# A SwiGLU feed-forward kernel: one weight load moves from SyncE's queue to GpSimd, behind a wait

## The chip, the core and the metric

The kernel runs on one core of a Trainium2 chip. The metric is the device time of one execution in microseconds (us), as a median over several executions. In the profile PE is TensorE's matmuls, PEld its weight loads, DVE is VectorE, ACT is ScalarE, POOL is GpSimd and SP is SyncE; a name with q behind it (SPq, POOLq) is that engine's instruction queue, which also issues DMAs.

## What is computed

```python
B, S, D, F = 1, 2048, 512, 1376     # all bfloat16

def reference(x, w_gate, w_up, w_down):
    g = silu(x @ w_gate)             # [2048, 1376]
    u = x @ w_up                     # [2048, 1376]
    return (g * u) @ w_down          # [2048, 512]
```

## The kernel before

The 2048 tokens are worked in four chunks of 512, numbered c = 0 to 3. F is cut into tiles of 128 columns: ten whole tiles (0 to 9) and a rest of 96. Each whole tile of each chunk has a gate group G and an up group U. A group accumulates over four slices of D (the loop variable `dk`) into one PSUM bank of 128 partitions by 512 columns. Each product is issued as two matmuls, one for each half of the 128 output partitions (`m` is 0 or 64). ScalarE takes silu of the gate bank into `sg_sb` (L291), and VectorE multiplies it with the up bank into `hT_sb` (L305). When all four chunks are through, the rests of F are worked (kinds X and Y), and then the down projection with `wd_sb` gives the output rows, which SyncE stores.

The order of groups on TensorE is written out in the plan: for each chunk tile 0, tile 1, then tiles 2 and 3 together (both gates, then both ups), then tiles 4 to 9 one by one. Chunk 0 has a special beginning: its first 256 tokens arrive untransposed in `xn_sb`, TensorE transposes them (L374, L382), and tiles 0 and 1 are computed in pieces of 256 and 128 tokens as the parts of x arrive. From the gates of tile 2 on every matmul is 512 columns wide.

The weights lie in `w_sb`. They are loaded in slabs: `slabs = [(0, 2), (2, 4), (4, 6), (6, 8), (8, NFT)]`, where the pair is the first tile and the one behind the last. Slab a has one load of gate columns, named `wg` with its first tile (wg0, wg2, wg4, wg6, wg8), and one of up columns (wu0, wu2 and so on); `load_w` (L98) issues either. A load of two tiles is 256 KB: 128 partitions, four slices of D, 512 bytes each. Each load has a semaphore of its own that reaches 16 when all of it has landed. Before its first matmul with a load TensorE waits for that semaphore (`need`, L317 and in `gu_step`).

The DMA issues before the change, each engine's in the order of its queue:

- ScalarE: wg0, ahead of its first activation.
- SyncE: the untransposed x (`xn`, L114), wu0, two transposing loads of x for the rest of chunk 0 (x0b and x0c, L93), wg2, wu2, wg4, wu4, wg6, wu6, wg8, wu8, a small load wut, the transposing loads x1, x2 and x3 of the other chunks, the down weights (wd, four wdt, wdl), and much later the stores of the output.
- GpSimd: no DMA. It makes one iota (L274), from which VectorE makes the identity for the transposes.

There are no loops at run time; all queues are written out when the program is built.

Of the kernel before, what the change touches and what calls it, by code (L numbers as in the profile page):

```python
# [13 lines left out]
def bass_standalone__swiglu_ffn__prompt_kernel(nc, x, w_gate, w_up, w_down, out):  # L14
    _, S, D = x.shape
    F = w_gate.shape[1]
    P = 128
# [29 lines left out]
    with ExitStack() as es:  # L47
# [33 lines left out]
        loads = {}  # L81

        def load_sem(name):
            loads[name] = sem(f"s_{name}")
            return loads[name]
# [6 lines left out]
        def load_x(eng, name, t0, t1):  # L92
            eng.dma_start_transpose(  # L93
                xT_sb[:, :, t0:t1], xf[t0:t1, :]
            ).then_inc(load_sem(name), 16)

        def load_w(eng, name, src, base, f0, f1):
            eng.dma_start(  # L98
                w_sb[:, :, base + f0:base + f1],
                src[:, f0:f1].rearrange("(k p) f -> p k f", p=P),  # L100
            ).then_inc(load_sem(name), 16)

        slabs = [(0, 2), (2, 4), (4, 6), (6, 8), (8, NFT)]
        slab_of = {ft: a for a, b in slabs for ft in range(a, b)}

        def load_slab(eng, a, b):
            load_w(eng, f"wg{a}", w_gate, 0, a * P, min(b * P, F))
            load_w(eng, f"wu{a}", w_up, UPH, a * P, min(b * P, F - 32))

        def loads_on_scalar(act):  # L110
            load_w(act, "wg0", w_gate, 0, 0, slabs[0][1] * P)

        def loads_on_sync(sp):
            sp.dma_start(  # L114
                xn_sb[:, :, :].rearrange("p j d -> p (j d)"), xf[0:HT, :].rearrange("(p j) d -> p (j d)", j=NXN)
            ).then_inc(load_sem("xn"), 16)
            load_w(sp, "wu0", w_up, UPH, 0, slabs[0][1] * P)
            load_x(sp, "x0b", HT, HT + P)
            load_x(sp, "x0c", HT + P, SC)
            for a, b in slabs[1:]:  # L120
                load_slab(sp, a, b)
            load_w(sp, "wut", w_up, F - (F - 32), F - 32, F)
            for c in range(1, NSC):
                load_x(sp, f"x{c}", c * SC, (c + 1) * SC)
            sp.dma_start(
                wd_sb[:, 0:NFF, :], w_down[0:NFF * P, :].rearrange("(k p) d -> p k d", p=P)
            ).then_inc(load_sem("wd"), 16)
            for c in range(NSC):
                sp.dma_start(
                    wdt_sb[R * c:R * (c + 1), :, :], w_down[NFF * P:F, :].rearrange("(q p) d -> p q d", p=R)  # L130
                ).then_inc(load_sem(f"wdt{c}"), 16)
            sp.dma_start(wdl_sb[:, :], w_down[NFF * P:F, LASTA:D]).then_inc(load_sem("wdl"), 16)
# [86 lines left out]
        for dk in range(KD):  # L219
            g = add_group("T", dk=dk)  # L220
            eng = "DA"[dk % 2]
# [19 lines left out]
        for at in range(NST):  # L241
# [4 lines left out]
            for c0, c1 in [(0, LASTA), (LASTA, LASTB), (LASTB, D)] if end else [(0, D)]:  # L246
                g = add_group("O", t=t, c0=c0, c1=c1, c=c)
                (quads[j] if c0 == 0 else last).append(g)
                eng = "A" if (end and c0 == 0) or (j < TPC - 1 and c % 2) else "D"
                op = add_op(  # L250
                    eng, g, kind="copy", out=o_sb[ob][:, c0:c1], src=g["bank"][:, 0:c1 - c0],
# [6 lines left out]
        def rows_of(t):  # L258
            if t < NXN:
                return of[0:HT, :].rearrange("(p j) d -> j p d", j=NXN)[t]  # L260
            return of[t * P:(t + 1) * P, :]

        def on_sync(sp):
            loads_on_sync(sp)
            for t, c0, c1, ob, eng, n in stores:
                if (c0, c1) == (0, LASTA):
                    continue
                sp.wait_ge(s_A if eng == "A" else s_D, n)
                sp.dma_start(rows_of(t)[:, c0:c1], o_sb[ob][:, c0:c1]).then_inc(s_out[ob], 16)
            for i in range(NST, NST + NOS):  # L270
                sp.wait_ge(s_out[i % NOS], 16 * n_store[i % NOS])

        def on_gpsimd(pool):
            pool.iota(  # L274
                diag[:, :], pattern=[[-1, P]], base=0, channel_multiplier=1,
            ).then_inc(s_I, 1)

        def on_scalar(act):
            loads_on_scalar(act)
            act.activation(adummy[:, 0:4], zero_c, ACT.Silu)  # L280
            for op in act_ops:
                act.wait_ge(s_P, op["g"]["at"] + 1)
                if op["kind"] == "silu":
                    if op["free"]:
                        act.wait_ge(s_D, op["free"])
                    fn = ACT.Silu
                else:
                    if op["stored"][1]:
                        act.wait_ge(*op["stored"])
                    fn = ACT.Copy  # L290
                act.activation(op["out"], op["src"], fn).then_inc(s_A, 1)  # L291
            for t, c0, c1, ob, eng, n in stores:
                if (c0, c1) == (0, LASTA):
                    act.wait_ge(s_A, n)
                    act.dma_start(rows_of(t)[:, c0:c1], o_sb[ob][:, c0:c1]).then_inc(s_out[ob], 16)
# [215 lines left out]
                ).then_inc(s_P, 1)  # L511

        on_sync(nc.sync)
        on_gpsimd(nc.gpsimd)
        on_scalar(nc.scalar)
        on_tensor(nc.tensor)
        on_vector(nc.vector)

# [27 lines left out]
```

## Time and profile before

| what | value |
|---|---|
| three executions | 120.25, 119.51, 119.6 us; median 119.6 us |
| the profiled execution | 120.67 us, of which the profile's span is 119.3 us |
| PE busy | 116.6 us, 98% of the span |
| PEld, DVE, ACT busy | 66.4, 43.4, 35.5 us |
| POOL busy | 0.4 us, five instructions |
| HBM read | 4.81 MB |
| mean granted TensorE clock | 1.000 |

The span runs from the first to the last recorded instruction; what lies around it, here 1.4 us, belongs to the launch and the end of the execution. "Busy" for PE includes a matmul's modelled end, so that overlapping matmuls leave no gap even where they run slowly. DMA times are given from the start of the issuing instruction to the last landing.

### The profile page before, as it was taken

The page shows a single profiled execution, that of the slowest core. Times are in us where ns is not written, and L with a number is a line of the kernel's source. Part 1 is how long each engine was busy: PE and PEld are TensorE (multiplying, and loading weights), DVE is VectorE, ACT ScalarE, POOL GpSimd, SP SyncE. Part 2 cuts the span into 40 slices and gives each one's busy share as a digit, 9 for nine tenths or more (in the row PEclk, how much of TensorE's full clock was granted, in tenths as well). Part 3 has the DMA queues.
Part 4 walks back from the last instruction along what each step waited for, and adds up shares of the span by engine and source line. Part 5 has one row for each costly group of instructions (what it writes and reads, how often), then busy time and mean ns, then how long its engine had stood idle before and what let it go on. Part 6 is the DMA issues. An engine that isn't in the chain of part 4 may idle for free.

```text
span 119.3 us, 2992 instructions
## 1 busy us (share of the span) xinstructions
PE 116.6 (98%) x1343; PEld 66.4 (56%) x1344; DVE 43.4 (36%) x68; ACT 35.5 (30%) x61; POOL 0.4 (0%) x5
## 2 busy tenths in 40 slices
PE   7999999999999999999999999999999999999993
PEld 2796555555555555555555555554444444464452
DVE  0103534442534452444352444369800040214331
ACT  4225243265242365232454323470000030213001
POOL 1000000000000000000000000000000000000000
DMA  3999999991000000000000000000000023023612
GB/s 80 278 283 335 194 253 228 269 295 23 0 5 0 0 0 0 5 0 5 0 5 0 0 0 0 5 0 0 5 0 5 0 86 95 0 92 106 204 44 88
DMA packets 17596, 8.92 MB, mean 75 GB/s; under 512 B 8624, under 2 KB 17456, under 8 KB 17584
## 3 DMA queue, kind: packets, MB, share of 16 engines
q1 hardware_dynamic: 16912, 8.38, 27.1%
q10 hardware_dynamic: 672, 0.36, 1.0%
q8 instruction: 10, 0.16, 0.6%
q14 instruction: 2, 0.02, 0.0%
HBM read 4.81 MB, written 2.10 MB: 58 GB/s over the span
## 4 chain that ended last, share of the span: by engine, by line
PE 98%; issue 0%; DVE 0%
PE psum L345 59%; PE psum L456 24%; PE psum L433 7%; PE psum L409 3%; PE psum L359 2%; PE psum L420 1%; PE psum L382 0%; PE psum L374 0%; PE psum L364 0%; DVE o_sb L309 0%; PE psum L508 0%
## 5 line engine op out<-in xcount | busy, mean ns | idle before, releaser
L345 PE MATMUL psum<-xT_sb,w_sb 128*64 128x512 bf16 (+2 forms) x680 | 71.0, 371 | 0.0
L345 PEld LDWEIGHTS psum<-xT_sb,w_sb 128*64 128x64 bf16 x680 | 43.0, 112 | 27.1
L305 DVE TENSOR_TENSOR hT_sb<-sg_sb,psum 128x512 bf16<-128x512 f32 x40 | 27.5, 687 | 41.5 <-PE psum L345 36.6
L291 ACT ACTIVATE sg_sb<-psum 128x512 f32<-128x512 f32 x40 | 23.8, 596 | 41.6 <-PE psum L345 41.6
L456 PE MATMUL psum<-wd_sb,hT_sb 32*128 32x512 bf16 x480 | 26.9, 374 | 0.0
L456 PEld LDWEIGHTS psum<-wd_sb,hT_sb 32*128 32x128 bf16 x480 | 13.0, 93 | 13.0 <-issue 0.4
L309 DVE CAST o_sb<-psum 128x512 bf16<-128x512 f32 (+1 forms) x11 | 6.4, 603 | 25.2 <-PE psum L456 19.9
L291 ACT ACTIVATE o_sb<-psum 128x512 bf16<-128x512 f32 (+1 forms) x7 | 3.7, 580 | 33.0 <-PE psum L456 25.9
L433 PE MATMUL psum<-wd_sb,hT_sb 128*128 128x512 bf16 (+2 forms) x59 | 8.7, 307 | 0.2 <-issue 0.2
L433 PEld LDWEIGHTS psum<-wd_sb,hT_sb 128*128 128x128 bf16 x60 | 4.6, 98 | 4.6 <-issue 0.4
L305 DVE TENSOR_TENSOR ht_sb<-sgy_sb,yu_sb 32x512 bf16<-32x512 f32 x8 | 5.5, 683 | 0.4
L409 PE MATMUL psum<-xT_sb,w_sb 128*64 128x512 bf16 x32 | 4.2, 379 | 0.0
L305 DVE TENSOR_TENSOR ht_sb<-sgx_sb,psum 32x512 bf16<-32x512 f32 x4 | 2.8, 691 | 3.5 <-ACT sgx_sb L291 3.5
L291 ACT ACTIVATE sgx_sb<-psum 32x512 f32<-32x512 f32 x4 | 2.4, 588 | 4.5 <-PE psum L409 4.5
L359 PE MATMUL psum<-const-bfloat16-1.0 128*128 128x512 bf16 x6 | 2.7, 623 | 0.8 <-PEq L531 0.8
L456 PE MATMUL psum<-wdt_sb,ht_sb 32*128 32x512 bf16 (+1 forms) x48 | 3.3, 371 | 0.0
L409 PEld LDWEIGHTS psum<-xT_sb,w_sb 128*64 128x64 bf16 x32 | 2.0, 110 | 1.4
L291 ACT ACTIVATE sgy_sb<-psum 64x512 f32<-64x512 f32 x4 | 2.4, 590 | 0.1
L456 PEld LDWEIGHTS psum<-wdt_sb,ht_sb 32*128 32x128 bf16 x48 | 1.3, 93 | 1.3
L420 PE MATMUL psum<-xT_sb,w_sb 128*64 128x512 bf16 x16 | 1.9, 379 | 0.0
L359 PEld LDWEIGHTS psum<-const-bfloat16-1.0 128*128 128x128 bf16 x6 | 0.7, 133 | 1.9 <-issue 1.9
L280 ACT ACT_TABLE_LOAD x1 | 1.3, 1283 | 1.2 <-PEq L531 1.2
(21 smaller groups left out, 7.6 us busy)
## 6 DMA issues: line engine op xcount, KB each, us to landing
out_dram<-o_sb SPq DMA_DIRECT2D x15, 128.0 KB, 1.8
wd_sb<-in_w_down_dram SPq DMA_DIRECT2D x1, 1280.0 KB, 8.9
w_sb<-in_w_up_dram SPq DMA_DIRECT2D x4, 256.0 KB, 4.0
w_sb<-in_w_gate_dram SPq DMA_DIRECT2D x3, 256.0 KB, 3.9
wdt_sb<-in_w_down_dram SPq DMA_DIRECT2D x4, 96.0 KB, 7.2
w_sb<-in_w_gate_dram SPq DMA_DIRECT2D x1, 352.0 KB, 6.2
w_sb<-in_w_up_dram SPq DMA_DIRECT2D x1, 320.0 KB, 6.3
w_sb<-in_w_gate_dram ACTq DMA_DIRECT2D x1, 256.0 KB, 3.6
```

What stands on the lines that cost most here:

```text
L280: act.activation(adummy[:, 0:4], zero_c, ACT.Silu)
L291: act.activation(op["out"], op["src"], fn).then_inc(s_A, 1)
L305: ins = dve.tensor_tensor(op["out"], op["a"], op["b"], ALU.mult)
L309: ins = dve.tensor_copy(op["out"], op["src"])
L345: ins = pe.matmul(g["bank"][m:m + HC, n0:n1], lhsT=w_sb[:, dk, col + m:col + m + HC], rhs=xT_sb[:, dk, c * SC + n0:c * SC + n1], start=(dk ...
L359: pe.matmul(banks[NB - 1][:, 0:width], lhsT=ones_w, rhs=ones_m[:, 0:width], start=True, stop=True)
L409: ins = pe.matmul(g["bank"][m:m + HC, :], lhsT=w_sb[:, dk, XC0 + m:XC0 + m + HC], rhs=xT_sb[:, dk, c * SC:(c + 1) * SC], start=(dk == 0), ...
L420: ins = pe.matmul(g["bank"][y0:y1, :], lhsT=w_sb[:, dk, YC0:YC0 + 64], rhs=xT_sb[:, dk, c * SC:(c + 1) * SC], start=(dk == 0), stop=(dk == ...
L433: ins = pe.matmul(g["bank"][:, 0:c1 - c0], lhsT=hT_sb[:, fk, t * P:(t + 1) * P], rhs=wd_sb[:, fk, c0:c1], start=(start and fk == 0), stop= ...
L456: ins = pe.matmul(g["bank"][:, 0:c1 - c0], lhsT=h(r, g["t"]), rhs=w[R * r:R * (r + 1), c0:c1], start=(start and n == 0), stop=final, tile_ ...
```

## The change

The load wg2 leaves SyncE's queue. GpSimd issues it instead, behind its iota and behind a wait for wg0's semaphore to reach 16. SyncE goes from x0c straight to wu2. ScalarE's program is now built before GpSimd's, because wg0's semaphore is made there; each engine's own queue is otherwise as it was. The matmuls, their order and their waits by name are the same.

```diff
-        def load_slab(eng, a, b):
-            load_w(eng, f"wg{a}", w_gate, 0, a * P, min(b * P, F))
+        def load_slab(eng, a, b, gate=True):
+            if gate:
+                load_w(eng, f"wg{a}", w_gate, 0, a * P, min(b * P, F))
             load_w(eng, f"wu{a}", w_up, UPH, a * P, min(b * P, F - 32))
...
             for a, b in slabs[1:]:
-                load_slab(sp, a, b)
+                load_slab(sp, a, b, gate=a != slabs[1][0])
...
             pool.iota(
                 diag[:, :], pattern=[[-1, P]], base=0, channel_multiplier=1,
             ).then_inc(s_I, 1)
+            pool.wait_ge(loads["wg0"], 16)
+            load_w(pool, "wg2", w_gate, 0, slabs[1][0] * P, slabs[1][1] * P)
...
         on_sync(nc.sync)
+        on_scalar(nc.scalar)
         on_gpsimd(nc.gpsimd)
-        on_scalar(nc.scalar)
         on_tensor(nc.tensor)
         on_vector(nc.vector)
```

## The prediction

> **What bounds the kernel now.** I read the chain that ended last first, then TensorE's waits, then SyncE's queue in the first ten microseconds, then the moment at which the moved load is needed. The page says who sets the end:
>
> ```profile
> PE 116.6 (98%) x1343; PEld 66.4 (56%) x1344; DVE 43.4 (36%) x68; ACT 35.5 (30%) x61; POOL 0.4 (0%) x5
> ...
> PE 98%; issue 0%; DVE 0%
> ```
>
> The chain followed back from the last instruction is TensorE almost alone. Its waits, in the view of who waited for whom with PE alone:
>
> ```profile
> PE psum L359 <- PEq L531: 0.8, 1, 0.8
> PE psum L433 <- issue: 0.2, 1, 0.2
> ```
>
> Neither is a wait for a DMA: the first is the start of the program, the second is in the down projection. This view can hide a short wait under a matmul's modelled end, so I also followed the starts of the weight loads and matmuls one by one through the first 13 us. From 4.4 us on they follow one another without a hole. The one load that gates TensorE is wg0, and with it the transposed x: wg0 is issued at 0.73 and takes 3.6, so it lands at 4.33, and the first weight load of L345 starts at 4.39 (the last copy of x that it needs ends only shortly before, so both decide). From a landing to the weight load that waits for it there are thus 0.06 us.
>
> SyncE's queue in that time, as the timeline has it:
>
> ```profile
> 1.67 2.57 SPq L93 DMA_TRANSPOSE xT_sb<-in_x_dram  x2
> 4.28 0.58 SPq L98 DMA_DIRECT2D w_sb<-in_w_gate_dram  x1
> 4.91 0.51 SPq L98 DMA_DIRECT2D w_sb<-in_w_up_dram  x1
> 5.46 0.51 SPq L98 DMA_DIRECT2D w_sb<-in_w_gate_dram  x1
> ```
>
> The issue at 4.28 is wg2. The view of w_sb for the windows round this issue and round ScalarE's wg0 gives their landings (the last column of the first line is the form):
>
> ```profile
> L98 ACTq DMA_DIRECT2D w_sb<-in_w_gate_dram x1: 463/463/463, 0.7 to 0.7; - x1
> ...
> DMA to landing us min/median/max: 3.6/3.6/3.6
> ...
> L98 SPq DMA_DIRECT2D w_sb<-in_w_gate_dram x1: 581/581/581, 4.3 to 4.3; - x1
> ...
> DMA to landing us min/median/max: 3.5/3.5/3.5
> ```
>
> So wg2 lands at 4.28 + 3.55 = 7.83 (the landing records give the second digit). When is it needed? Its matmuls are the first that are 512 columns wide, and the groups by form between 9.07 and 9.10 us hold just the change from 256 to 512:
>
> ```profile
> L345 PE MATMUL psum<-xT_sb,w_sb 128*64 128x256 bf16 x4 | 0.4, 273 | 0.0
> L345 PE MATMUL psum<-xT_sb,w_sb 128*64 128x512 bf16 x2 | 0.4, 379 | 0.0
> ```
>
> The first of them starts at 9.08, and the weight load that carries the wait for wg2 at 8.97. It therefore lands 1.1 us before it is needed. This spare time is what the change spends.
>
> **The change, part by part.**
>
> *SyncE loses one issue.* Everything behind it is issued 4.91 - 4.28 = 0.63 us earlier. This is worth nothing as long as nothing waits for it. The cover is TensorE's own work: wu2 lands at 8.57 and is first needed at 10.6 (behind two gate tiles of 0.86 each, the distance of the silus at 10.15 and 11.02); wg4 lands at 9.32 and is needed at 12.5; x1 lands at 17.13 and chunk 1 starts at 23.75. Each load has over 1.9 us to spare, and the last kernel loads lie further from their use. A gain is excluded by PE's idle time of 0.0 in front of the L345 matmuls: 0.0 us.
>
> *GpSimd gets a wait.* It is met at 4.33 and, with the 0.06 from above, lets the next instruction go at 4.39. Queued behind the waiting instruction is only the load itself; the iota, for which VectorE waits, stands ahead of it and ends at 1.05. Only TensorE waits for the load, at L345. So the wait costs 0.11 us of the spare time against SyncE's issue at 4.28.
>
> *GpSimd issues the load.* The trace of before shows no DMA issued by GpSimd, so its time from issue to landing has to be bounded. The nearest row is wg0: the same 256 KB in the same shape, the first DMA of its queue, with SyncE's queue busy beside it: 3.6 us. That gives 4.39 + 3.6 = 7.99. From below, the shortest row of a full-width transfer is the output store of 128 KB:
>
> ```profile
> out_dram<-o_sb SPq DMA_DIRECT2D x15, 128.0 KB, 1.8
> ...
> w_sb<-in_w_gate_dram SPq DMA_DIRECT2D x1, 352.0 KB, 6.2
> w_sb<-in_w_up_dram SPq DMA_DIRECT2D x1, 320.0 KB, 6.3
> ```
>
> With 1.8 it lands at 6.19. From above, the longest load of w_sb, 320 KB that stood behind others in its queue, took 6.3: 10.69. I take 3.6, because bytes, shape and an empty own queue agree. TensorE's weight load could then go at 8.05, and goes at 8.97 anyway: stall 0, with 0.92 us left. The upper end gives 10.69 + 0.06 - 8.97 = 1.78 us of stall, the lower one none. A stall on PE is paid in full, since 98% of the span behind it is PE and no later row of PE has idle time to give back; the silus and products of the tile would be late by the same amount and find their engines idle (1.13 us before each silu, 1.04 before each product).
>
> The Trainium skill, "DMA: Bandwidth & Descriptors", section "Anatomy of one DMA — SWDGE (gpsimd) path", gives a fit for a DMA issued by GpSimd of 2.0 us plus the bytes over 436 GB/s; by that the estimate is 2.6 us and the landing 6.99, earlier than by the row. No run so far shows it, and the sum does not use it.
>
> *The two queues now run side by side.* In SyncE's queue wg2 stood behind x0c, which lands at 6.18. Now wg2 can move its bytes beside x0b, x0c and wu2. If wg2 went wholly ahead of them, its 256 KB at the 341 GB/s of the stretch from 8.5 to 9.5 us would be 0.77 us: x0c would land at 6.95, and its first matmul waits at 7.49. Cost 0, cover 0.54 us. If all that was in flight at 4.39 were slowed to half, x0c would land at 4.39 + 2 x 1.79 = 7.97, 0.54 us late with the 0.06.
>
> *VectorE against GpSimd.* If the two got in each other's way, it would be while VectorE works, and it has a hole there: its last copy of x ends at 4.48 and its next instruction starts at 8.69.
>
> ```profile
> 8.69 0.69 DVE L305 TENSOR_TENSOR hT_sb<-sg_sb,psum 128x512 bf16<-128x512 f32 x1 [4.20 <-ACT sg_sb L291]
> ```
>
> **Sum.** 0.0 (SyncE) + 0.0 (wait and issue, hidden in the 1.1 us) + 0.0 (sharing) on the profiled execution's 120.67 us. That one is 1.07 us above the median of the three runs, so the forecast for the median is 119.6. Over 1%, or 1.2 us, is about what a measurement of this kernel can tell from no change.
>
> One thing makes the spare time smaller than it looks. Between 4.4 and about 6.7 us the 256-wide matmuls start every 0.107 us on average (pairs 0.213 apart), afterwards every 0.055, although the granted clock reads 1.00 throughout. If another execution reached the fast pace from the start, 2.3 / 2 = 1.15 us would be gone and wg2 needed at 7.82. The landing of 7.99 would then cost 0.2 us. The unprofiled runs lie 0.4 to 1.2 us below the profiled one, which would fit such an earlier change of pace, or merely profiling. That stall is within the 1%.
>
> **The rivals.**
>
> *1. The wait moves to TensorE, slower.* GpSimd's way from issue to landing is longer than ScalarE's, and TensorE stands in front of the gates of tile 2. It decides from 8.97 - 0.06 - 4.39 = 4.5 us on (3.4 us if the pace is fast from the start). For it: wg2's margin is the smallest of all loads, and the load is 512 pieces of 512 bytes, with nothing in the trace to show how fast GpSimd issues them. Against it: the nearest row is 0.9 us shorter. With 6.3 us it gives 119.6 + 1.8 = 121.4; to be over 1.2 us it needs a landing after 10.1. Should GpSimd first fetch code, it would be worse: one more 6.3 us ahead of the 3.6 lands at 14.3, a stall of 5.4 and 125.0. The trace speaks against that, since the two configuration instructions at 0.74 and 0.77 are followed by the iota at 0.82. (The Trainium skill, "GPSIMD Engine Reference", section "Instruction dispatch", states some 6 us for the first call of a freshly loaded kernel; the row does not show it for the iota, and for a DMA no run shows it.)
>
> *2. The earlier loads are worth something, faster.* If TensorE were held by loads behind wg2 in ways the starts don't show, they could give back at most 0.63 us: 119.0. Against it: 0.0 idle before L345, and every margin above 1.9 us.
>
> *3. Sharing hurts chunk 0's x.* x0c late by 0.54 us: 120.1. Against it: until x0c lands, the DMA queues move only 118 GB/s (5.5 to 6.5 us), so there is room.
>
> *4. It does not do what it says.* If GpSimd's transfer is served behind SyncE's full queue, the load lands when, say, wu6 does, at 13.1, and the time is 119.6 + 4.2 = 123.8. Nothing in the trace speaks for it; ScalarE's wg0 was not held behind SyncE's two transposing loads, which were issued but landed after it.
>
> **How the numbers follow.** No stall or less than 1.2 us of it, 119.6 likeliest: 0.68. Sharing, still within 1%: 0.03. Rival 1 over 1.2 us: 0.22, with 0.04 of it beyond 121.5. Rival 4: 0.02. Rival 2: 0.04 together with chance, some of it under 1%. Rest 0.01, slower. Faster 0.03, same 0.72, slower 0.25. The range runs from 119.1, for rival 2 and the scatter of the three runs, up to 121.4, the upper bound of the issue; about 2 in 10 lie outside.
>
> **What would show it.** In the profile after: a GpSimd issue of w_sb at 4.4 us with a landing before 8.9; wu2's issue at 4.28; the first 512-wide matmuls at about 9.1; TensorE's waits without a line for w_sb; the span within 1 us of 119.3. I am wrong if the landing of wg2 is after 8.9 and the first 512-wide matmul follows it at once, if that matmul is late although the load is there, or if the wide matmuls keep their place and the end moves nevertheless.

## The result, and the profile after

The changed kernel takes 121.51 us in the median of six executions, the kernel before 119.81 (six as well). The ratio is 1.0127, with a 95% interval of 1.0095 to 1.0159: slower by 1.3%, some 1.5 us. One of the six, 123.46 us at a lower granted clock, is not in the ratio (the other five have a median of 121.31 us), and in the experiments below one of the ten of the extra load, 122.31 us, is left out of its ratio. The profiled execution took 121.71 us with a span of 120.4, against 120.67 and 119.3 before.

The busy times of the page, and its chain that ended last:

```profile
PE 116.6 (97%) x1344; PEld 61.4 (51%) x1344; DVE 43.4 (36%) x68; ACT 35.5 (29%) x61; POOL 1.3 (1%) x6
...
PE 90%; DMA 7%; issue 0%; DVE 0%
PE psum L348 55%; PE psum L459 24%; DMA w_sb<-in_w_gate_dram 7%; PE psum L436 7%; PE psum L412 3%; PE psum L423 1%; DVE o_sb L312 0%; PE psum L511 0%
```

TensorE's busy time is the same to a tenth, but a DMA now stands in the chain: a load of gate columns. (The 7% are the whole way of two such loads, wg2 and before it wg0, for which GpSimd waited; they are not the loss. L345 of before is L348 here.) TensorE's waits name the place, with the total, the number and the longest:

```profile
PE psum L348 <- DMA w_sb<-in_w_gate_dram: 1.1, 1, 1.1
PE psum L362 <- PEq L534: 0.8, 1, 0.8
```

There is one new wait, once, for 1.1 us. The timeline from 4.2 us on shows which load it is (start, length, engine, what; the bracket is the idle time before it and what ended that):

```profile
4.30 0.58 SPq L98 DMA_DIRECT2D w_sb<-in_w_up_dram  x1
4.44 4.27 PEld L348 LDWEIGHTS psum<-xT_sb,w_sb 128*64 128x64 bf16 x72
4.68 0.87 POOL L98 DMA_DIRECT2D w_sb<-in_w_gate_dram  x1 [3.61 <-DMA w_sb<-in_w_gate_dram]
10.11 5.97 PEld L348 LDWEIGHTS psum<-xT_sb,w_sb 128*64 128x64 bf16 x58 [1.40 <-DMA w_sb<-in_w_gate_dram]
```

SyncE issues wu2 at 4.30 as planned, and GpSimd issues wg2 at 4.68, once wg0 has landed (4.39). TensorE runs through tiles 0 and 1 and then stands before the gates of tile 2 until 10.11. The DMA issues of the window round GpSimd's give its time to landing, and the groups by form from 10.0 to 10.2 us show that the first 512-wide matmuls follow at once:

```profile
w_sb<-in_w_gate_dram POOLq DMA_DIRECT2D x1, 256.0 KB, 5.4
```

```profile
L348 PE MATMUL psum<-xT_sb,w_sb 128*64 128x512 bf16 x2 | 0.4, 403 | 1.1 <-DMA w_sb<-in_w_gate_dram 1.1
```

So wg2 lands at 4.68 + 5.38 = 10.06, where it landed at 7.83 before. The last pair of matmuls before the gap starts at 8.69, and pairs stood 0.11 apart, so TensorE would have gone on at 8.80; it stands 1.3 us, of which the view hides a part under the modelled end of that pair. The DMA queues of the stretches 5.6 to 7.8 and 7.8 to 9.7 us (share of the 16 engines' time at the end) show when its bytes move; q0 is GpSimd's queue, q1 SyncE's:

```profile
q1 hardware_dynamic: 872, 0.42, 82.5%
...
q1 hardware_dynamic: 784, 0.39, 68.0%
q0 software_dynamic: 80, 0.26, 34.1%
```

GpSimd's issue is over at 5.55, and its first packet moves at 7.85. There lies most of the delay.

Nothing is given back or lost later. From the first 512-wide matmul to the end of the span it is 110.27 us before (119.342 - 9.075) and 110.29 after (120.397 - 10.106). This tail is 110.27 to 110.30 us in eleven of the thirteen traces of this case (in the other two TensorE waits again later), so the span is the start of that matmul plus 110.28, and spans of other executions can be turned into that start.

### The profile page after: what moved, and what is told of

It reads as the page before. It is cut to its first block, busy times and chain, and to the rows that moved or that the text cites. A ratio compares the mean times of both kernels' runs of the same rounds, so it can differ in the third digit from the quotient of the medians.

```text
span 120.4 us, 2993 instructions
## 1 busy us (share of the span) xinstructions
PE 116.6 (97%) x1344; PEld 61.4 (51%) x1344; DVE 43.4 (36%) x68; ACT 35.5 (29%) x61; POOL 1.3 (1%) x6
## 4 chain that ended last, share of the span: by engine, by line
PE 90%; DMA 7%; issue 0%; DVE 0%
PE psum L348 55%; PE psum L459 24%; DMA w_sb<-in_w_gate_dram 7%; PE psum L436 7%; PE psum L412 3%; PE psum L423 1%; DVE o_sb L312 0%; PE psum L511 0%
## 5 line engine op out<-in xcount | busy, mean ns | idle before, releaser
L348 PE MATMUL psum<-xT_sb,w_sb 128*64 128x512 bf16 (+2 forms) x680 | 70.8, 370 | 1.1 <-DMA w_sb<-in_w_gate_dram 1.1
L348 PEld LDWEIGHTS psum<-xT_sb,w_sb 128*64 128x64 bf16 x680 | 38.6, 112 | 32.5 <-DMA w_sb<-in_w_gate_dram 1.4
L412 PEld LDWEIGHTS psum<-xT_sb,w_sb 128*64 128x64 bf16 x32 | 1.8, 110 | 1.6
```

The lines of the kernel that those rows point to most:

```text
L348: ins = pe.matmul(g["bank"][m:m + HC, n0:n1], lhsT=w_sb[:, dk, col + m:col + m + HC], rhs=xT_sb[:, dk, c * SC + n0:c * SC + n1], start=(dk ...
L412: ins = pe.matmul(g["bank"][m:m + HC, :], lhsT=w_sb[:, dk, XC0 + m:XC0 + m + HC], rhs=xT_sb[:, dk, c * SC:(c + 1) * SC], start=(dk == 0), ...
```

## Where the spare time had gone

The profiled execution before had 1.1 us between the landing and the need. Thirty-one executions of the kernel before, run beside the first four experiments, had spans from 118.1 to 119.3 us; 21 of them had 118.5 or less. By the tail, TensorE came to the gates of tile 2 at 7.8 to 9.0 us, in two thirds of the executions at 8.2 or before. The profiled one (119.3) was among the slowest. The changed kernel's five comparable executions had 119.7 to 120.4, which puts that point at 9.4 to 10.1.

What moves it is the moment at which the 256-wide matmuls go over from a pair every 0.213 us to one every 0.109. In the eleven traces with the warm-up matmuls this was at 6.74 (before), 6.15 (after), about 6.1 in three more, 5.7 in two, 4.9 in one, and in three the fast pace was there from the first of these matmuls at 4.4; in the two without warm-up (below) it was at 7.2. The granted clock read 1.00 in all. Two stretches of the kernel before show the pace and the clock (length, PE busy with the number of matmuls, four more engines, the clock, the DMA engines; the second stretch also holds sixteen matmuls of 128 columns):

```profile
4.40:6.60 2.20, 2.20 (x24) 2.18 (x24) 0.09 (x1) 0.46 (x2) 0.00 (x0) 1.00 1.03 200
6.60:9.07 2.47, 2.47 (x54) 2.47 (x52) 0.38 (x1) 0.81 (x2) 0.00 (x0) 1.00 1.08 319
```

A change of pace 1 us earlier brings the gates of tile 2 forward by 0.5: with the change at 4.9 and no wait they start at 8.18, with 6.74 at 9.08. (The Trainium skill, "TensorE: Matmul & The Clock Gate", Part 1, describes a clock gate that opens after a busy window of about 3.4 us, in a window that runs free of the kernel's start and so shifts from run to run; the scatter here agrees with that in kind, the granted clock of the profile does not show it.)

## The experiments

Theory A at the start: GpSimd's way from issue to first packet is long by itself. Theory B: its packets are held behind SyncE's backlog on the DMA engines. Theory C: a load outside SyncE's queue costs by its presence. All eleven runs are variants of the two kernels.

**No wait.**

```diff
-            pool.wait_ge(loads["wg0"], 16)
```

> GpSimd issues wg2 right behind its iota, without waiting for wg0. Theory A (GpSimd's own way from issue to first packet is about 3.2 us whatever else runs, as 4.68 to 7.85 in the changed kernel): issue at about 1.1, first packet at about 4.3, landing at 6.5 or before, no stall, 119.8 us. Theory B (the packets are held behind SyncE's backlog on the DMA engines): first packet not before 6 us, landing 8 to 9, time between 119.8 and 120.5. Theory C (a load outside SyncE's queue is what costs, wait or not): 121.5.

Issue at 1.34, first packet at 4.34, landing at 6.09, no wait of TensorE for it. The 3.0 us to the first packet are close to A's 3.2, and B's first packet after 6 us did not come. The time is 120.32 us, ratio 1.0045 (1.0022 to 1.0069). C falls: most of the loss is gone with the wait. But not all, and the ten executions lie close together (spans 118.8 to 119.2), with none at the 118.2 that the kernel before often reaches. The early load shares the engines with chunk 0's x: x0c lands at 7.16 instead of 6.18. The trace shows no wait for it, but an estimate does: TensorE comes to x0c at 7.49 in the trace before and would come 1.15 earlier at the fast pace, so that x0c would be 0.9 us late and the shortest span 119.0 instead of 118.1. This is the sharing of the prediction's third rival, in a place where the change itself does not have it (there x0c landed at 6.23).

**ScalarE issues it.**

```diff
-            pool.wait_ge(loads["wg0"], 16)
-            load_w(pool, "wg2", w_gate, 0, slabs[1][0] * P, slabs[1][1] * P)
...
+                if op["at"] == 2:
+                    load_w(act, "wg2", w_gate, 0, slabs[1][0] * P, slabs[1][1] * P)
```

> ScalarE instead of GpSimd issues wg2, behind its two copies of x, so at about 4.95, later than GpSimd's 4.68; SyncE still goes straight to wu2. Theory A: ScalarE's way is short (3.6 for wg0), landing at about 8.5, stall 0 to 0.5, 119.8 to 120.3 us. Theory B, that SyncE's backlog holds any other queue: landing near 10, about 121.4. Theory C: 121.5.

The issue came at 4.58, earlier than expected and 0.10 before GpSimd's, and the load landed after 4.2 us, at 8.79. The time is 120.49, ratio 1.0048 (1.0025 to 1.0071). From almost the same moment ScalarE's load is thus there 1.3 us before GpSimd's 10.06, and B's landing near 10 did not come. It is not there at SyncE's 7.83, though: it was issued 0.30 later, behind wu2's issue, and took 0.66 longer, and the time lies above A's range, with more than a third of the loss left. In this trace the first 512-wide matmul starts at 8.84, 0.04 us after the landing and 0.25 later than the pace of the pairs would have it; PE's waits do not show this, for the reason named above.

**GpSimd loads the ups instead.**

```diff
-            load_w(pool, "wg2", w_gate, 0, slabs[1][0] * P, slabs[1][1] * P)
+            load_w(pool, "wu2", w_up, UPH, slabs[1][0] * P, slabs[1][1] * P)
```

(SyncE's `load_slab` leaves out wu2 and keeps wg2.)

> GpSimd issues wu2 behind the same wait and SyncE keeps wg2. If the loss is only the lateness of one load, wu2 lands at about 10.1, is needed 1.7 us after the gates, at 10.0 to 10.6, and the time is 119.8 to 120.0. If a GpSimd load costs by its presence (contention, launch, end of the execution), the time stays near 121.4.

wu2 lands at 9.40, 4.8 us after its issue; in that trace its weight load goes at 10.26 and does not wait. 120.18 us, ratio 1.0022 (0.9993 to 1.0051): no difference that can be told, and at most 0.5%. The same slow load costs little or nothing where there is room for it. The median is a little above the expected 120.0.

**An extra load.** GpSimd loads into a spare buffer behind the same wait, SyncE keeps everything.

```diff
+        spare = sb("spare", [P, KD, 2 * P], BF16)
...
-                load_slab(sp, a, b, gate=a != slabs[1][0])
+                load_slab(sp, a, b)
...
-            load_w(pool, "wg2", w_gate, 0, slabs[1][0] * P, slabs[1][1] * P)
+            pool.dma_start(
+                spare[:, :, :], w_gate[:, slabs[1][0] * P:slabs[1][1] * P].rearrange("(k p) f -> p k f", p=P),
+            ).then_inc(load_sem("spare"), 16)
...
+            need("spare")
             need("wd")
```

> SyncE keeps all its loads; GpSimd, behind the same wait, loads a second copy of wg2's columns into a spare buffer that nothing reads; TensorE waits for it once, before the down projection. Lateness alone: 119.8, since the extra 256 KB only push later loads back by 0.8 us and these have more than that to spare. If the presence of a GpSimd load costs: 120.5 to 121.5.

120.14 us, ratio 1.0017 (0.9989 to 1.0044). A launch or end cost of a GpSimd load does not show: what lies around the span is 1.31 us here and 1.33 in the kernel before. The expectation missed one thing: wg2 lands 0.5 us later beside the extra bytes (8.35), and in the profiled execution, at the fast pace from the start, TensorE waits 0.3 us for it and 0.2 for wu2.

**SyncE keeps quiet.**

```diff
+            sp.wait_ge(loads["wg2"], 16)
             for a, b in slabs[1:]:
                 load_slab(sp, a, b, gate=a != slabs[1][0])
...
-        on_sync(nc.sync)
         on_scalar(nc.scalar)
         on_gpsimd(nc.gpsimd)
+        on_sync(nc.sync)
```

(SyncE's program is built behind GpSimd's, because wg2's semaphore is made there.)

> The changed kernel, but SyncE waits after x0c until wg2 has landed before it issues wu2, so that from 6.3 us on the DMA engines carry nothing but GpSimd's load. This is for the times of that load, not for the kernel's time, which the late wu2 must lengthen by some 2 us. Theory A (a fixed way from GpSimd's issue to its first packet): issue at about 4.65, first packet 2.7 to 3.2 us later, at 7.4 to 7.8, then 0.8 us of bytes instead of 1.8, landing at 8.4 to 8.8. Theory B (held behind SyncE's backlog): first packet at about 6.2, as soon as x0c is through, landing at about 7.2.

Each theory is half right. The load's time to landing, and the queues of the stretches 4.7 to 6.2 and 6.2 to 7.6 us:

```profile
w_sb<-in_w_gate_dram POOLq DMA_DIRECT2D x1, 256.0 KB, 3.4
```

```profile
q1 hardware_dynamic: 922, 0.22, 79.8%
...
q0 software_dynamic: 80, 0.26, 72.1%
```

The issue starts at 4.64 and takes 0.87 as always; the first packet moves at 6.22, 1.58 us after the start, and not 2.7 to 3.2. That is against A. It is the moment of B: x0c lands at 6.22 too. But SyncE's last packet had ended by 5.76, and the landing is 7.99, not 7.2. Nor were the engines full in the changed kernel all the time that its load could have moved: from 6.25 to 7.0 us SyncE's packets filled 63% of their time (they were full from 7.0 on), and GpSimd's first came at 7.85. GpSimd's load does not wait for the landing of the SyncE load issued just before it either: in the runs with the ups and with the extra load its first packet moves 0.58 and 0.92 us before that landing. And VectorE did not stand in its way: in the changed kernel VectorE does nothing from 4.53 to 8.34. So B as a queue behind bytes does not explain that delay, or not all of it; that SyncE has issued loads does bring it about. One execution was timed, 120.73 us; SyncE's late loads lengthen it (TensorE waits 0.9 us for wu2).

**A quarter of the load, two ways.** First the slice of D with number 0 by GpSimd (128 pieces of 512 bytes), the rest by SyncE; then 64 of the 256 columns (512 pieces of 128 bytes), the rest by SyncE. GpSimd's part is shown; in both, SyncE's part has a semaphore of its own (wg2r), for which TensorE waits as well.

```diff
+            pool.dma_start(
+                w_sb[:, 0:1, slabs[1][0] * P:slabs[1][1] * P],
+                w_gate[0:P, slabs[1][0] * P:slabs[1][1] * P].rearrange("(k p) f -> p k f", p=P),
+            ).then_inc(load_sem("wg2"), 16)
```

```diff
+            load_w(pool, "wg2", w_gate, 0, 2 * P, 2 * P + HC)
```

> The changed kernel, but GpSimd loads only the first quarter of wg2 (the slice of D with number 0: 128 pieces of 512 bytes instead of 512); SyncE loads the other three quarters where wg2 stood before the change. If the way to the first packet is fixed, the issue still takes about 0.9 us and the first packet comes 2.7 to 3.2 us after its start, landing at about 8. If it grows with the pieces, the issue takes 0.3 us or less and the first packet comes within 1 us, landing before 6.3.

> As the quarter run, a quarter of wg2's bytes through GpSimd and the rest through SyncE where wg2 stood, but cut the other way: 64 of the 256 columns of all four slices, so 512 pieces of 128 bytes instead of 128 pieces of 512 bytes. If the number of pieces sets GpSimd's way, the issue takes about 0.87 us and the first packet comes at 7.3 or later, as with the whole load. If the bytes set it, 0.67 us and about 6.4, as with the quarter.

GpSimd's issue in the timelines, the quarter by slice and then the quarter by columns:

```profile
4.62 0.67 POOL L283 DMA_DIRECT2D w_sb<-in_w_gate_dram  x1 [3.55 <-DMA w_sb<-in_w_gate_dram]
```

```profile
4.61 0.88 POOL L98 DMA_DIRECT2D w_sb<-in_w_gate_dram  x1 [3.54 <-DMA w_sb<-in_w_gate_dram]
```

The bytes are the same, 64 KB. With 128 pieces the issue takes 0.67 us, the first packet moves at 6.43, and the part lands at 7.55. With 512 pieces it takes 0.88 like the whole load, the first packet moves at 7.31, and the part lands at 8.67. It is the number of pieces, not the bytes, that lengthens the way; nor is it that the pieces are short, for the whole load, 512 pieces of 512 bytes, is no quicker. (One thing differs besides: SyncE's part has 384 pieces beside the first quarter and 512 beside the second, and lands at 7.13 and 7.28. What that adds is not shown.) The expectation for the small number was too low: 1.8 us to the first packet, not under 1. One execution was timed of each, 120.16 and 120.32 us; in the second TensorE waits 0.6 us for GpSimd's part.

**SyncE waits only for x0c.** This came from a new theory D: the way is 1.6 us with SyncE's queue quiet, and longer when SyncE issues its next loads meanwhile.

```diff
+            sp.wait_ge(loads["x0c"], 16)
             for a, b in slabs[1:]:
                 load_slab(sp, a, b, gate=a != slabs[1][0])
```

> The changed kernel, but SyncE waits after x0c until x0c has landed (about 6.2) before it issues wu2 and goes on. New theory D: GpSimd's way to the first packet is about 1.6 us with SyncE's queue quiet and gets 1.1 to 1.6 us longer when SyncE has issued the next loads meanwhile. Then the first packet comes at 6.2 to 6.4, wg2 lands at 8.0 to 8.3, and most of the loss is gone: 119.8 to 120.3 us, though every load of SyncE behind x0c is issued 1.9 us later. Theory A (a fixed 2.7 to 3.2 us): first packet at 7.4 to 7.8, landing 9.4 or later, 121.0 to 121.6.

First packet at 6.26 (x0c lands at 6.24), landing at 8.14, as D said and A did not. The time was 120.53, ratio 1.0052 (1.0014 to 1.0090), a little more than expected. A likely reason is wu2, which now lands at 10.19: TensorE waits for no load in this trace, but at the fast pace from the start it would come to the ups of tile 2 at about 9.6 (7.9 and two tiles of 0.86), as an estimate. No run here shows it.

All GpSimd loads together, in us:

| run | pieces | SyncE's next loads | issue starts | to first packet | lands |
|---|---|---|---|---|---|
| changed kernel | 512 | issued from 4.3 on | 4.68 | 3.17 | 10.06 |
| ups instead | 512 | issued from 4.3 on | 4.64 | 2.67 | 9.40 |
| extra load | 512 | issued from 4.3 on | 4.59 | 2.84 | 10.15 |
| changed, unwarmed (below) | 512 | issued from 4.3 on | 4.62 | 2.82 | 9.45 |
| quarter by columns | 512 | issued from 4.3 on | 4.61 | 2.70 | 8.67 |
| no wait | 512 | x0b and x0c from 1.7, wu2 from 4.3 | 1.34 | 3.00 | 6.09 |
| quarter by slice | 128 | issued from 4.3 on | 4.62 | 1.82 | 7.55 |
| quarter by slice, timed (below) | 128 | issued from 4.3 on | 4.66 | 1.83 | 7.79 |
| SyncE keeps quiet | 512 | after wg2 | 4.64 | 1.58 | 7.99 |
| SyncE waits for x0c | 512 | after x0c | 4.67 | 1.59 | 8.14 |

In the last two rows the first packet coincides with the landing of x0c, so their 1.6 us is an upper bound for the way with nothing beside it.

**Take the hurry away.** Both kernels without their six warm-up matmuls, so that TensorE comes to tile 2 later.

```diff
-N_WARM = 6
+N_WARM = 0
```

> The kernel before without its six warm-up matmuls (they multiply ones into a bank that is overwritten). TensorE then changes to its fast pace later, the gates of tile 2 are needed later, and every execution loses by it: 0.5 to 2 us over the kernel before, 120.5 to 121.8. It is the reference for the next run.

> The changed kernel without the six warm-up matmuls. If the change costs only what wg2's landing (9.4 to 10.1) exceeds the moment TensorE comes to it, most of its loss is hidden here, because TensorE comes to it at 9.2 to 11: 0 to 0.6 us above the unwarmed kernel before, instead of the 1.5 to 1.7 us with warm-up. If the change costs something by itself, the 1.5 us stay.

The medians are 121.36 (before) and 121.43 us (after), four executions each, with ratios to the kernel before of 1.0136 (1.0083 to 1.0189) and 1.0165 (1.0133 to 1.0197). The two differ by 0.3% where the warmed kernels differ by 1.3%; their intervals overlap, and with their widths the difference could be up to 0.9%. In the profiled execution after, wg2 lands at 9.45 and the first 512-wide matmul starts at 9.49. PE's waits have no line for it, but the view of w_sb has one for the weight load:

```profile
who waited for it (us, times):
  PEld psum L348: 0.3, 1
```

The last pair before starts at 9.19 and pairs stand 0.11 apart, so TensorE still loses 0.2 us here, against 1.3 in the profiled execution with warm-up. That fits a change that costs only what the landing exceeds TensorE's arrival.

**A version without the loss.** The quarter by slice, timed.

> The quarter kernel (GpSimd loads slice 0 of D of wg2, SyncE the other three), timed. Both parts landed at 7.6 or before in its trace, before the 7.8 of the kernel before and before TensorE can come to them at its fastest (about 7.9). So the loss of the changed kernel should be gone: 119.5 to 120.0, the same as before within 0.4%. If a GpSimd load costs something by itself, 120.2 or more. A gain over the kernel before is not expected, since TensorE's own pace sets the moment.

120.08 us, ratio 1.0010 (0.9989 to 1.0031): the loss is gone within what can be told, with a quarter of the load still on GpSimd (its part landed at 7.79 this time, and the gates of tile 2 start at 8.18 without a wait). No variant was faster than the kernel before.

## Why the prediction was wrong

- *What bounds the kernel, and the price of a stall:* right. TensorE's chain sets the end, the stall is paid in full (first 512-wide matmul 1.03 us later, span 1.06 later), and no DMA but wg2 matters.
- *SyncE's earlier issues, 0.0:* right. wu2 was issued 0.6 us earlier and landed at 7.89 instead of 8.57, and nothing got faster. That everything behind wg2 is issued earlier was wrong, though: SyncE's later issues took up to 1.37 us each, x1 was issued 0.66 later than before, and of the loads behind wg2 in w_sb wu2 alone landed earlier (wg6 lands at 12.89 instead of 10.92). None of them was late for TensorE.
- *GpSimd's wait, 0.06 from landing to the next instruction:* mis-sized. It was 0.29 (4.39 to 4.68).
- *GpSimd's issue to landing, "I take 3.6":* this is the step that failed. It was 5.38. The row of ScalarE's wg0 had the bytes and the shape but another engine's way and another moment. The run with ScalarE parts the two: from 4.58 on, beside SyncE's loads, ScalarE's own load of this shape took 4.21, so about 0.6 of the 1.78 us that were missed are the moment and 1.2 are GpSimd. The Trainium skill's fit ("DMA: Bandwidth & Descriptors", section "Anatomy of one DMA — SWDGE (gpsimd) path"), 2.6 us by its figures, was further off still: 3.35 with SyncE quiet, 4.8 to 5.6 for the 256 KB loads issued at 4.6 beside SyncE's. The upper end, 6.3, did hold it.
- *Together:* wg0 landed 0.06 later, the wait took 0.23 more and the load 1.78 more, which is the 2.07 us between the expected landing at 7.99 and 10.06.
- *The spare time of 1.1 us:* right for the profiled execution, wrong for the median. The prediction saw that a faster start would bring the need to 7.82 and that the unprofiled runs lay lower, and priced it at 0.2 us on top of the wrong landing. With the need at 7.9 in many executions and the landing at 9.4 to 10.1, the two errors add up to the 1.5 us measured, not to the 1.1 of the profiled pair. The sum took its time from the median of the executions and its spare time from the slowest of them.
- *Sharing, and VectorE against GpSimd, 0.0 each:* right. x0c landed at 6.23, 0.05 later than before, and GpSimd's issue took 0.87 us in the hole in VectorE's work.
- *The rivals:* the first one happened, with its place and its point of decision (3.4 to 4.5 us of issue to landing; 5.4 came). It had 0.22 of the chance above 1.2 us, and its price of 1.8 us from the longest row gave 121.4, close to the measured 121.51. That nearness is luck: the price rests on a landing at 10.69 and a need at 8.97, and most executions had both earlier. A fetch of code ahead of the load, priced at 125.0, did not come: the issue took 0.87 us. The second, third and fourth did not happen: nothing got faster, x0c landed at 6.23, and wg2 was not held to the end of SyncE's queue. The reason given against the fourth showed little, for wg0 was issued at 0.73 and SyncE's transposing loads only from 1.67 on; what SyncE had issued before did matter in the end.

## What to carry to other kernels

The spare time of a load is a difference of two moments that both scatter; before it is spent, put the profiled execution among the other executions, here by span less a constant tail, and take the earliest need. A load moved to another engine should be costed with a row of that engine; where there is none, the uncertainty is the result, and the forecast should stand nearer to the end that stalls when the margin is the smallest in the kernel. If a load has to go to GpSimd, give it few pieces, or a place with more room than the 2.2 us by which it landed later here. And a wait that PE's own view does not show can stand at its weight loads: look there too.

## What the runs showed of the hardware

GpSimd's load of 512 pieces needed at most 1.6 us from issue to first packet with SyncE's queue quiet (two traces), and 2.7 to 3.2 when SyncE issued its own loads in the same time (six traces), though in the changed kernel SyncE's packets filled only 63% of the DMA engines' time from 6.25 to 7.0 us. Beside SyncE's loads 64 KB took 1.8 us from issue to first packet in 128 pieces (two traces) and 2.7 in 512 (one). What the two queues share there, ahead of the packets, no view of the profile shows, and it stays open. Once moving, GpSimd's packets were 4 KB (159 ns at the median), where SyncE's are up to 512 bytes in these loads, and its 256 KB took 1.4 to 1.8 us beside SyncE's weight loads and 1.2 to 1.3 with SyncE quiet or transposing x, from the start of the first 4 KB packet to the start of the last. From wg0's landing to GpSimd's next instruction it was 0.29 us, where TensorE's weight load stood 0.04 to 0.06 behind the landing that it waited for.
